# The first two gate/up steps of block 0, whole or in two token halves

## The chip, the cores and the metric

The kernel runs on one core of one Trainium2 chip. The metric is the device time of one execution in microseconds. A profile of one execution gives, for each engine, when every instruction began and how long it took; times inside it count from the start of its span. TensorE is called PE (its weight loads PEld), VectorE DVE, ScalarE ACT, GpSimd POOL, and the queue of SyncE that issues most transfers SP.

## The reference, cut to what matters

```python
xn = _layernorm(x)                                  # x: 2048 tokens x 512
B  = (_gelu(xn @ w_gate) * (xn @ w_up)) @ w_down    # w_gate, w_up: 512 x 1376
A  = 2 * Re(scan(Lam_bar, xn @ B_bar^T) @ Cmat^T) + xn * Dskip
return x + A + B
```

A state-space layer A (a complex linear recurrence over the 2048 tokens) and a gated feed-forward layer B read the same normalised input, and their sum is added to x.

## The kernel before

**Tiling.** The 2048 tokens are four blocks of 512, and a block is four token tiles of 128 (tile 0 to tile 3). `XNT[b]` holds the normalised block transposed, with the 512 features in four groups of 128 partitions. The 1376 columns of `w_gate` and `w_up` are steps of 128, numbered `ft` 0 to 10 (the last is 96 wide). A gate/up step (`GU`, line 844) is four matmuls of 128x512 for the gate and four for the up projection, one PSUM bank each; then ACT takes the gelu of the gate bank (line 859) and copies the up bank (863), and DVE multiplies the two (865).

**The start.** Block 0 does not wait for its own normalisation. `ks` and `GT_mm` (lines 702 and 713) run steps 0 to 6 of block 0 on centred but unscaled tokens, token tile by token tile: for tile `j` and column range `u` one bank takes gate and up side by side, and `GT_evac` scales both while it empties the bank, ACT with a gelu (line 722), then DVE with a product (725). A gelu writes one of three `GG` slots, which the product then frees. The last ten of these units are, in order, tile and range (3,0) in bank 6, (3,1) in 7, (0,2) in 0, (0,3) in 1, (1,2) in 2, (1,3) in 3, (2,2) in 4, (2,3) in 5, (3,2) in 0 and (3,3) in 7. Ranges 0 to 2 are 256 columns of gate and of up, range 3 is 128.

**Meanwhile** DVE normalises the four tiles of block 0 (line 635), and each is transposed into `XNT[0]` by a DMA of its own (`TR`, line 737), issued one behind the other on SP. Steps 7 to 10 of block 0, `GU(0, [7, 8, 9, 10])`, read `XNT[0]`: step 7 writes banks 2 and 3, step 8 banks 4 and 5, step 9 banks 6 and 7, and step 10 (line 818) banks 0 and 1. So a unit's bank must be emptied before the step that comes next in it.

**Other work at the start.** The layer's small parameters are loaded and transposed by a DMA (line 516). POOL raises e to one of them (558), DVE multiplies that by another (559, `th`), and from there DVE builds the phase tables (562 to 607). Block 1 is loaded, normalised and transposed (616 to 635, 737), `BU(0)` and `BU(1)` (line 750) multiply blocks 0 and 1 by the recurrence's input matrix; the first four units of `BU(1)` are already in two halves, tiles 0 and 1 first.

**What sets the order.** Each call adds an operation with an estimated duration to a list; what it must wait for follows from the buffers that it reads and writes. PE and SP keep the order of the calls. For DVE, ACT and POOL, a planner (`Sched.schedule`) chooses the order from the estimated durations, and it plans the whole kernel anew when one operation changes. Each engine then runs its list strictly as planned, with semaphore waits between engines. In a matmul's dependencies `XTr(b)` stands for the four tile transposes of a block:

```python
XTr = lambda b: XTk[b]
PE(f, d_pe([c1 - c0] * 4), wdeps(Wc, ft) + rd, [BANK[bank]], "GU%d" % b)
```

Of the kernel before, what the change touches and what calls it, by code (L numbers as in the profile page):

```python
# [348 lines left out]
NT, NB, KD, KP, KF = 16, 4, 4, 4, 11  # L349
# [6 lines left out]
def d_pe(n_list):  # L356
    return sum(n / 2.4 + 2.5 for n in n_list)
def d_dve_tt2x(n): return 100.0 + 0.52 * n
# [4 lines left out]
def d_act(n, ptr=0): return 190.0 + 0.833 * n + 90.0 * ptr  # L363
# [3 lines left out]
def build(nc, ins, out):  # L367
    with ExitStack() as es:
# [11 lines left out]
        WG = A.alloc("WG", [KD, F], BF16)  # L380
        WU = A.alloc("WU", [KD, F], BF16)
# [4 lines left out]
        WGc = [Buf("WGc%d" % i, "sbx", 10 * i, 10 * i + 1) for i in range(KD + 2)]  # L386
        WUc = [Buf("WUc%d" % i, "sbx", 100 + 10 * i, 101 + 10 * i) for i in range(KD + 2)]
# [30 lines left out]
        XTk = [[Buf("XT%d_%d" % (b, i), "xt", 4 * b + i, 4 * b + i + 1) for i in range(4)] for b in range(NB)]  # L418
        XT0 = XTk[0]
        XTr = lambda b: XTk[b]  # L420
# [128 lines left out]
        def next_bank():  # L549
            b_ = rstate["n"] % 8  # L550
            rstate["n"] += 1
            return b_
# [56 lines left out]
        def tables_act(after_gelu):  # L609
            t = ACT(lambda e: e.activation(SC16.ap, FRC.ap, ACTF.Sin, scale=SIN_SCALE), d_act(16) + 1300, [FRC], [SC16], "sin16", after=after_gelu)  # L610
            t = ACT(lambda e: e.activation(COST.ap, A1.ap, ACTF.Sin, bias=HPI.ap, scale=-SIN_SCALE), d_act(2048), [A1, HPI], [COST], "cost", after=[t])
            return ACT(lambda e: e.activation(SINT.ap, F1.ap, ACTF.Sin, scale=-SIN_SCALE), d_act(2048), [F1], [SINT], "sint", after=[t])  # L612
# [56 lines left out]
        def SKIP(b):  # L669
            for tt in range(4 * b, 4 * b + 4):  # L670
                xs = XN[tt % 8]
                V(lambda e, tt=tt, xs=xs: e.tensor_tensor(XD[tt].ap, xs.ap, DSKB.ap, ALU.mult),
                  d_dve_tt2x(512), [xs, DSKB], [XD[tt]], "skip")
# [156 lines left out]
            S.dma(lambda e: e.dma_start_transpose(HTt[k2][ft].ap.rearrange("p (j t) -> p j t", j=4), HR.ap),  # L830
                  1.2 * 128 * 1024, reads=HRp, writes=[HTt[k2][ft]], tag="tr_h%d" % b, issue=1200.0)

        def GU(b, fts=None):
            k2 = b % 2
            fts = list(range(KF) if fts is None else fts)
            banks = {}

            def mm(ft, W, Wc, bank, c0, c1, rd):
                m = FROWS[ft]

                def f(e):
                    ins_ = None
                    for dk in range(KD):
                        ins_ = e.matmul(PS[bank][0:m, c0:c1], W.ap[:, dk, 128 * ft:128 * ft + m], XNT[b].ap[:, dk, c0:c1],  # L844
                                        start=(dk == 0), stop=(dk == KD - 1))
                    return ins_
                PE(f, d_pe([c1 - c0] * 4), wdeps(Wc, ft) + rd, [BANK[bank]], "GU%d" % b)

            for ft in fts:
                m = FROWS[ft]  # L850
                if m < 128:
                    GU_rest(b)
                    continue
                banks[ft] = (next_bank(), next_bank())
                bg, bu = banks[ft]
                kk = (KF * b + ft) % 3
                for (W, Wc, bank) in zip((WG, WU), (WGc, WUc), banks[ft]):
                    mm(ft, W, Wc, bank, 0, 512, XTr(b))
                GATE["last_gelu"] = ACT(lambda e, bg=bg, kk=kk, m=m: e.activation(  # L859
                    GG[kk].ap[0:m, :], PS[bg][0:m, :], ACTF.Gelu_apprx_tanh),  # L860
                    d_act(512), [BANK[bg]], [GG[kk]], "gelu", after=GATE["before_gelu"])
                S.order_behind(GATE["last_gelu"], GATE.pop("evBu", None))
                ACT(lambda e, bu=bu, kk=kk, m=m: e.activation(UPB[kk].ap[0:m, :], PS[bu][0:m, :], ACTF.Copy),  # L863
                    d_act(512), [BANK[bu]], [UPB[kk]], "evU")
                V(lambda e, kk=kk, m=m, ft=ft, k2=k2: e.tensor_tensor(  # L865
                    HTt[k2][ft].ap[0:m, :], GG[kk].ap[0:m, :], UPB[kk].ap[0:m, :], ALU.mult),
                  d_dve_tt2x(512), [GG[kk], UPB[kk]], [HTt[k2][ft]], "hmul")
# [155 lines left out]
        LN(1, [0, 1]); LN(1, [2, 3])  # L1023
        TR(1)
        SKIP(0)
        GU(0, [7, 8, 9, 10])
        GATE["before_gelu"] = [tables_act([GATE["last_gelu"]])]
        SKIP(1)
        BU(0)
# [8 lines left out]
        late_loads()  # L1038
        scale_C()
        GU(1, [0, 1, 2, 10, 3, 4, 5, 6, 7, 8, 9])  # L1040
        BU(2)
        CHAIN(2)
        DN(0, True)
        LN_act(3); SKIP(3)
        GU(2, [0, 1, 2, 10, 3, 4, 5, 6, 7]); TR(3); GU(2, [8, 9])
        BU(3)
        CHAIN(3)
# [9 lines left out]
def bass_parallel_sum__ssm_conv_s5__geglu_ffn__prompt_kernel(  # L1057
    nc: bass.Bass,
    A_x: bass.AP,
    A_Lambda_re: bass.AP,  # L1060
    A_Lambda_im: bass.AP,
    A_B_re: bass.AP,
    A_B_im: bass.AP,
    A_C_re: bass.AP,
    A_C_im: bass.AP,
    A_log_dt: bass.AP,
    A_Dskip: bass.AP,
    B_x: bass.AP,
    B_w_gate: bass.AP,
    B_w_up: bass.AP,  # L1070
    B_w_down: bass.AP,
    out: bass.AP,
):
    ins = {
        "A_x": A_x, "A_Lambda_re": A_Lambda_re, "A_Lambda_im": A_Lambda_im,
        "A_B_re": A_B_re, "A_B_im": A_B_im, "A_C_re": A_C_re, "A_C_im": A_C_im,
        "A_log_dt": A_log_dt, "A_Dskip": A_Dskip,
        "B_w_gate": B_w_gate, "B_w_up": B_w_up, "B_w_down": B_w_down,
    }
    build(nc, ins, out)  # L1080
# [28 lines left out]
```

## Time and profile before

| What | Value |
|---|---|
| Median time of 3 runs | 177.01 us (176.86 to 177.09) |
| Span of the profiled execution | 176.4 us, 2522 instructions |
| Busy: DVE, ACT, POOL | 91%, 54%, 6% of the span |
| Granted TensorE clock | 1.00 |
| Matmuls of line 844 (gate/up steps) | 264, 58.1 us busy |
| Matmuls of line 713 (units of block 0) | 40, 7.1 us busy |
| DMA share in slices of 4.4 us, first nine | 5 9 9 8 9 9 9 4 9 tenths |

A busy PE in this profile is one that has matmuls in flight. The time of a 512-column matmul is given as 379 ns, though the next one begins 216 ns later: they overlap, and it is the distance between starts that counts.

### The profile page before, as it was taken

The numbers are of one execution on the slowest core, as the hardware profiler recorded it, in microseconds if no ns is written. First come the engines' busy times: TensorE is split into PE (matmuls) and PEld (weight loads), VectorE is DVE, ScalarE is ACT, GpSimd is POOL, SyncE is SP. The second block draws the span as 40 slices with busy tenths as digits, with TensorE's granted clock in tenths as the row PEclk, the third lists the DMA queues.
The fourth block names the chain that finished last, engine by engine and source line by source line (L and its number), as shares of the span: only waits on it lengthen the run. The fifth ranks groups of instructions, "written<-read, shape, count | busy, mean of one in ns | idle before, by whom it ended". The sixth has DMA issues, their size and how long they took to land.

```text
span 176.4 us, 2522 instructions
## 1 busy us (share of the span) xinstructions
PE 172.9 (98%) x889; PEld 84.8 (48%) x889; DVE 159.7 (91%) x279; ACT 96.0 (54%) x187; POOL 10.7 (6%) x24
## 2 busy tenths in 40 slices
PE   8999899999999999999999999999999999999995
PEld 2646364744644444444644444444464444444454
DVE  5987989997999989979899999989999899999941
ACT  5476577999766899292676693000667970000000
POOL 3212120202000000001200000000000000000000
DMA  5998999495998000001115000002001000000221
GB/s 176 256 334 139 248 202 157 94 162 104 193 288 226 4 0 2 0 30 59 33 32 103 16 0 0 4 0 86 33 0 30 4 0 0 0 0 0 91 93 61
DMA packets 32421, 14.37 MB, mean 81 GB/s; under 512 B 23736, under 2 KB 32408, under 8 KB 32408
## 3 DMA queue, kind: packets, MB, share of 16 engines
q1 hardware_dynamic: 32096, 13.94, 34.6%
q10 hardware_dynamic: 312, 0.27, 0.4%
q8 instruction: 7, 0.11, 0.3%
q14 instruction: 6, 0.05, 0.1%
HBM read 6.46 MB, written 2.10 MB: 49 GB/s over the span
## 4 chain that ended last, share of the span: by engine, by line
PE 95%; DMA 2%; DVE 1%; issue 0%
PE PS L885 37%; PE PS L844 32%; PE PS L750 16%; PE PS L702 3%; PE PS L818 3%; DMA arena<-arena 2%; PE PS L934 2%; PE PS L713 1%; DVE arena L725 1%; PE PS L685 1%; DVE arena L903 0%; PE PS L941 0%
## 5 line engine op out<-in xcount | busy, mean ns | idle before, releaser
L885 PE MATMUL PS<-arena 128*128 128x512 bf16 (+3 forms) x323 | 66.2, 366 | 0.0
L844 PE MATMUL PS<-arena 128*128 128x512 bf16 x264 | 58.1, 379 | 0.9 <-DMA arena<-arena 0.9
L885 PEld LDWEIGHTS PS<-arena 128*128 128x128 bf16 (+1 forms) x323 | 30.9, 98 | 35.2
L844 PEld LDWEIGHTS PS<-arena 128*128 128x128 bf16 x264 | 25.7, 98 | 31.4 <-issue 1.1
L788 DVE TENSOR_TENSOR_SCAN arena<-arena 128x512 bf16<-128x512 f32 x32 | 38.9, 1254 | 0.0
L859 ACT ACTIVATE arena<-PS 128x512 bf16<-128x512 f32 x33 | 19.8, 599 | 26.8 <-DVE arena L903 16.7
L750 PE MATMUL PS<-arena 128*128 128x512 bf16 (+1 forms) x144 | 28.2, 355 | 0.0
L863 ACT ACTIVATE arena<-PS 128x512 bf16<-128x512 f32 x33 | 19.8, 599 | 5.6 <-PE PS L844 5.6
L750 PEld LDWEIGHTS PS<-arena 128*128 128x128 bf16 x144 | 14.1, 98 | 13.3
L877 ACT ACTIVATE PS<-arena 128x512 f32<-128x512 bf16 (+2 forms) x17 | 9.6, 581 | 19.7 <-DVE arena L903 19.0
L759 ACT ACTIVATE arena<-PS 128x512 bf16<-128x512 f32 x32 | 17.5, 595 | 1.8 <-PE PS L750 1.8
L903 DVE TENSOR_TENSOR arena<-PS,arena 128x512 bf16<-128x512 f32 (+2 forms) x17 | 10.9, 653 | 6.4 <-PE PS L885 6.4
L865 DVE TENSOR_TENSOR arena<-arena 128x512 bf16<-128x512 bf16 x33 | 13.2, 417 | 2.7 <-ACT arena L863 2.5
L777 DVE TENSOR_TENSOR arena<-arena 128x4096 bf16<-128x4096 bf16 (+1 forms) x5 | 9.2, 1858 | 0.4 <-ACT arena L612 0.4
L800 DVE TENSOR_TENSOR arena<-arena 128x4096 bf16<-128x4096 bf16 x4 | 9.2, 2288 | 0.1
L775 DVE TENSOR_TENSOR arena<-arena 128x4096 bf16<-128x4096 bf16 (+1 forms) x5 | 9.2, 1857 | 0.0
L801 DVE TENSOR_TENSOR arena<-arena 128x4096 bf16<-128x4096 bf16 x4 | 9.1, 2284 | 0.0
L722 ACT ACTIVATE arena<-PS,arena 128x256 bf16<-128x256 f32 (+1 forms) x16 | 6.6, 449 | 4.1 <-PE PS L702 2.4
L616 DVE BATCH_NORM_STATS2 arena<-arena 128x6 f32<-128x512 bf16 x12 | 7.8, 680 | 0.2 <-DMA arena<-in_A_x_dram 0.2
L713 PE MATMUL PS<-arena 128*128 128x512 bf16 (+1 forms) x40 | 7.1, 336 | 0.0
L725 DVE SCALAR_TENSOR_TENSOR arena<-PS,arena 128x256 bf16<-128x256 f32 (+1 forms) x16 | 6.3, 444 | 0.5 <-PE PS L702 0.5
L702 PE MATMUL PS<-arena 128*128 128x512 bf16 (+1 forms) x30 | 6.3, 351 | 0.0
(95 smaller groups left out, 124.2 us busy)
## 6 DMA issues: line engine op xcount, KB each, us to landing
out_dram<-arena SPq DMA_DIRECT2D x15, 128.0 KB, 1.7
arena<-in_A_x_dram SPq DMA_DIRECT2D x3, 512.0 KB, 5.4
arena<-in_B_w_down_dram SPq DMA_DIRECT2D x1, 1280.0 KB, 7.1
arena<-in_B_w_gate_dram SPq DMA_DIRECT2D x4, 128.0 KB, 3.3
arena<-in_B_w_up_dram SPq DMA_DIRECT2D x4, 128.0 KB, 3.4
arena<-in_B_w_gate_dram SPq DMA_DIRECT2D x1, 480.0 KB, 6.7
arena<-in_B_w_up_dram SPq DMA_DIRECT2D x1, 480.0 KB, 7.5
arena<-arena SPq DMA_TRANSPOSE x25, 3.1
```

The costliest lines, as they stand in the source:

```text
L702: PE(lambda e: e.matmul(dst, XCd(j, k), WGU[:, ws[0]:ws[-1] + 1, k, f0:f1], start=first, stop=k == KD - 1, skip_group_check=True), d_pe([w ...
L750: ins_ = e.matmul(PS[bank][:, 128 * j0:128 * j1], BBT[c][dk].ap[:, 128 * s:128 * (s + 1)], XNT[b].ap[:, dk, 128 * j0:128 * j1], start=(dk ...
L759: GATE["evBu"] = ACT(lambda e, bank=bank, k3=k3, s=s, c=c: e.activation(SSc[k3][s][c].ap, PS[bank][:, :], ACTF.Copy), d_act(512), [BANK[ba ...
L775: V(lambda e, s0=s0, s1=s1: e.tensor_tensor(TA.ap[:, s0:s1], ssb.ap[:, s0:s1], cos4[:, s0:s1], ALU.mult), d_dve_tt2x(1024 * step), [ss, CO ...
L788: V(lambda e, g=g, rb=rb, init=init: e.tensor_tensor_scan(g.ap, rb, g.ap, init, ALU.mult, ALU.add), d_dve_scan(512), [g, PA[RRr]] + ([CARc ...
L844: ins_ = e.matmul(PS[bank][0:m, c0:c1], W.ap[:, dk, 128 * ft:128 * ft + m], XNT[b].ap[:, dk, c0:c1], start=(dk == 0), stop=(dk == KD - 1))
L859: GATE["last_gelu"] = ACT(lambda e, bg=bg, kk=kk, m=m: e.activation(GG[kk].ap[0:m, :], PS[bg][0:m, :], ACTF.Gelu_apprx_tanh), d_act(512), ...
L863: ACT(lambda e, bu=bu, kk=kk, m=m: e.activation(UPB[kk].ap[0:m, :], PS[bu][0:m, :], ACTF.Copy), d_act(512), [BANK[bu]], [UPB[kk]], "evU")
L865: V(lambda e, kk=kk, m=m, ft=ft, k2=k2: e.tensor_tensor(HTt[k2][ft].ap[0:m, :], GG[kk].ap[0:m, :], UPB[kk].ap[0:m, :], ALU.mult), d_dve_tt ...
L877: ACT(lambda e: e.activation(PS[bank][:, c0:c1], X[tt].ap[:, c0:c1], ACTF.Copy), d_act(c1 - c0), [X[tt]], [BANK[bank]], "seed")
L885: ins_ = e.matmul(PS[bank][:, c0:c1], l_[:, 128 * j:128 * (j + 1)], r_[:, c0:c1], start=False, stop=last and n == len(ops) - 1, skip_group ...
L903: V(lambda e: e.tensor_tensor(OUTB[ko].ap[:, c0:c1], PS[bank][:, c0:c1], XD[tt].ap[:, c0:c1], ALU.add), d_dve_1x(c1 - c0), [BANK[bank], XD ...
```

## The change

The first two gate/up steps of block 0, steps 7 and 8, are each cut into two halves by tokens. First the half of tiles 0 and 1 is computed for both steps (columns 0 to 255 of banks 2, 3, 4 and 5), then the half of tiles 2 and 3 (columns 256 to 511 of the same banks). Steps 9 and 10 and all other blocks stay whole. It is meant to let PE begin these steps once the transposes of tiles 0 and 1 are there, without waiting for that of tile 3.

```diff
-        def GU(b, fts=None):
+        def GU(b, fts=None, halved=()):
...
+            for h in range(2 if halved else 0):
+                for ft in halved:
+                    if h == 0:
+                        banks[ft] = (next_bank(), next_bank())
+                    for (W, Wc, bank) in zip((WG, WU), (WGc, WUc), banks[ft]):
+                        mm(ft, W, Wc, bank, 256 * h, 256 * h + 256, XTk[b][2 * h:2 * h + 2])
             for ft in fts:
...
-                banks[ft] = (next_bank(), next_bank())
+                kk = (KF * b + ft) % 3
+                if ft not in halved:
+                    banks[ft] = (next_bank(), next_bank())
+                    for (W, Wc, bank) in zip((WG, WU), (WGc, WUc), banks[ft]):
+                        mm(ft, W, Wc, bank, 0, 512, XTr(b))
                 bg, bu = banks[ft]
-                kk = (KF * b + ft) % 3
-                for (W, Wc, bank) in zip((WG, WU), (WGc, WUc), banks[ft]):
-                    mm(ft, W, Wc, bank, 0, 512, XTr(b))
...
-        GU(0, [7, 8, 9, 10])
+        GU(0, [7, 8, 9, 10], halved=(7, 8))
```

On PE the 16 matmuls of 128x512 of steps 7 and 8 become 32 of 128x256. Nothing else in the calls differs, but the planner orders DVE, ACT and POOL anew.

## The prediction

> **What bounds the kernel now.** I read the page's busy shares first, then PE's waits, then the chain that ended last, then the timeline around the one wait that this gives.
>
> ```profile
> PE 172.9 (98%) x889; PEld 84.8 (48%) x889; DVE 159.7 (91%) x279; ACT 96.0 (54%) x187; POOL 10.7 (6%) x24
> ```
>
> PE has matmuls in flight for 98% of the span, so only PE's idle time can be won. Its waits, longest first (total, times, longest):
>
> ```profile
> PE PS L844 <- DMA arena<-arena: 0.9, 1, 0.9
> PE PS L934 <- PEq L1094: 0.8, 1, 0.8
> ```
>
> The second is the program's start. The first is the only wait in the body, and the chain says which transfer ends it (start, duration):
>
> ```profile
> 14.34 4.24 DMA arena<-arena
> 18.58 0.14 issue
> 18.72 5.34 PE PS L844 x24
> 24.06 1.32 PE PS L818 x16
> 25.38 13.85 PE PS L750 x80
> ```
>
> From 18.72 to 174.6 us the chain is PE alone: what starts earlier at 18.72 ends earlier at the end, if no later wait opens. The timeline shows what runs before it:
>
> ```profile
> 10.42 5.19 SPq L737 DMA_TRANSPOSE arena<-arena  x4
> 10.77 7.09 PE L713 MATMUL PS<-arena 128*128 128x512 bf16 x40
> ...
> 12.66 2.31 DVE L725 SCALAR_TENSOR_TENSOR arena<-PS,arena 128x256 bf16<-128x256 f32 x6
> ...
> 15.03 1.02 POOL L558 TENSOR_TENSOR arena<-arena 128x4 bf16<-128x4 f32 x1 [5.42 <-DMA arena<-arena]
> ...
> 16.16 0.16 DVE L559 TENSOR_TENSOR arena<-arena 128x4 f32<-128x4 bf16 x1 [1.19 <-POOL arena L558]
> 16.26 0.74 DVE L725 SCALAR_TENSOR_TENSOR arena<-PS,arena 128x256 bf16<-128x256 f32 x2
> ...
> 18.72 5.34 PE L844 MATMUL PS<-arena 128*128 128x512 bf16 x24 [0.86 <-DMA arena<-arena]
> ```
>
> SP issues the four tile transposes 1.3 us apart from 10.42; by the view of line 737, cut to each, they land 4.7, 3.8, 3.1 and 4.2 us after their starts: 15.1, 15.5, 16.1 and 18.58. PE starts its last unit matmul at 17.59 and is free at 17.70. So tiles 0 and 1 have been there for 2.2 us when PE turns to step 7, and it stands until 18.72 for tile 3: 1.02 us between issue slots (0.86 in the waits, which count the drain). That is the most the change can bring. Note the second feature: DVE stands 1.19 us before line 559, whose input comes from POOL, which waited for the parameters' transpose (line 516; started 7.75, landed 7.1 later, 14.9).
>
> **What the skill says.** The Trainium skill, "TensorE: Matmul & The Clock Gate", section Back-to-back issue gap, gives 262 cycles for 256 columns and 518 for 512 as isolated gaps: two halves cost 6 cycles more than a whole. The trace agrees: line 713's starts are 0.108 us apart at 256 columns and 0.216 at 512, with a 98 ns weight load beside each. "Perfetto Trace Analysis", section Tensor Engine Instruction, calls ACT, DVE and GpSimd strict FIFOs. The trace agrees: the product for unit (1,2) started at 16.26 although its gelu had ended at 15.41; line 559 stood ahead of it. The same page, section DMA Instruction - HWDGE, says that a DMA's profiled time leaves out the data movement; here 1.27 us of issue against 4.24 to landing, so I use landings.
>
> **The change part by part.**
>
> *Removed:* the wait for tile 3 ahead of steps 7 and 8, 1.02 us. Tiles 2 and 3 are now needed 1.7 us later (four half groups of 4 x 0.108), at 19.4 or after, when they have landed.
>
> *Added on PE:* 16 more matmuls and weight loads; from 0.108 against 0.216 the columns cost the same, so nothing.
>
> *Added as a wait, by the shorter steps:* banks 4 and 5 (units (2,2) and (2,3)) are needed after two half groups, 0.86 us, not after two whole ones. Before, the product for (2,2) ended at 18.00 and bank 4 was wanted at 20.45: no issue as DVE was ordered then.
>
> *Moved, and this decides:* the planner orders DVE and ACT anew. In the built program ACT first empties the tile 3 transposes (line 690) and then starts the gelus. PE issues those transposes until 9.69; with 0.27 us from PE to ACT, as from line 702 to the first gelu, line 690 starts at 9.96, and the first gelu at 10.44 (0.48 behind, as before) instead of 9.73. Its product starts at 11.03 instead of 10.32. Then come six more products (0.39 to 0.40 each), one normalisation (0.32) and one reciprocal (0.12), so the 7th product ends at 14.3, where the 8th had ended before. And line 559 now stands behind the 7th, where it stood behind the 10th. It still cannot start before 16.16 (landing 14.90 + 0.13 + POOL 1.02 + 0.11). So units (3,0), (0,2) and (0,3), done by 14.96 before, wait for it:
>
> | DVE after line 559 | starts | ends | why |
> |---|---|---|---|
> | (0,2) | 16.26 | 16.74 | 0.10 behind line 559, as before |
> | (3,0) | 16.66 | 17.13 | 0.40 a product |
> | (1,2) | 17.05 | 17.53 | the same |
> | (0,3) | 17.69 | 18.03 | its gelu needs the GG slot of (3,0): 17.13 + 0.08 + 0.37 + 0.11 |
> | line 562, (1,3) | 17.95 | 18.37 | 0.08, then 0.34 |
> | line 603 | 18.29 | | 0.26 behind |
> | (2,2) | 18.69 | 19.17 | its gelu needs the slot of (0,3): 18.03 + 0.08 + 0.47 + 0.11 |
>
> PE queues behind these. Unit (3,2) reuses bank 0, which (0,2) frees at 16.74; with 0.06 from DVE to PE (as at 3.69 to 3.75, line 962 to 685) it starts at 16.80, not 16.40: 0.40 lost, with all of PE behind it. It and (3,3) take 1.30, two half groups 0.86: PE reaches bank 4 at 18.96 and finds it free at 19.23: 0.27 more. Bank 5 follows in time, 0.40 later on DVE against 0.43 on PE. Six half groups (0.432 each) end at 21.82. Before, four whole groups from 18.72 ended at 22.18.
>
> Sum: -1.02 + 0.40 + 0.27 = -0.35 us by the parts, 22.18 - 21.82 = 0.36 by the ends: 177.01 - 0.36 = 176.65.
>
> *Further moves.* In block 1 the normalisation of tile 7 is now behind four table products (line 605, 0.66 each): 29.1 instead of 25.6. Its transpose is issued at about 29.6 and with the 3.05 it took before (27.51 to 30.56) lands at 32.6. `BU(1)` wants tiles 6 and 7 at 33.84 - 0.36 = 33.5: hidden by 0.7 to 0.9, where it was 3.3. The transfers behind it on SP come some 2.6 us later; PE needs none of them before 57 us, hidden behind line 844 of block 1. POOL's start order changes within 2.3 us, ahead of the first input's landing at 2.94: no cost.
>
> **The rivals.**
> - *The full gain, 176.0.* The banks are free in time and PE runs through: 17.70 + 8 x 0.432 = 21.16, 1.02 less. For it: only 0.5 us of earlier parameters suffice for most of it. Against it: the landing at 14.90 stands in a full DMA row (8 to 9 tenths).
> - *A new wait of equal size, 177.1.* PE's time now hangs on the parameters' landing plus a fixed chain, before on tile 3's landing; in the trace these lie 3.68 us apart. If parameters land 0.5 later, each of the table's rows moves with them: 0.36 - 0.5, slightly slower or the same. For it: nothing in DVE's list lies between to absorb it. Against it: SP and its transfers are unchanged up to there.
> - *Slower, 177.6.* The transpose of tile 7 takes 4.7 us, as tile 0's did: 29.6 + 4.7 + 0.14 = 34.4 against 33.5, 0.95 lost. For it: the margin shrinks from 3.3. Against it: the DMA row is down to 4 tenths from 30.9 on, and 3.05 was measured there.
>
> **How the numbers follow.** Chances: forecast 0.50, full gain 0.19, equal wait 0.18, slower 0.13. The threshold of 0.2% is 0.35 us, on which the forecast sits; I give 0.36 of its 0.50 to faster and 0.14 to the same, leaning to faster because the two added waits are priced with every latency at its full measured size. The equal wait gives 0.14 to the same and 0.04 to slower. Faster 0.55, same 0.28, slower 0.17. The range goes from the full gain to just past the equal wait, 176.0 to 177.3, leaving out most of the slow case.
>
> **What would show it.** In the changed profile: PE waits on DVE line 725 at about 16.8 (line 713, 0.3 to 0.4) and about 19.2 (line 844, 0.2 to 0.3), and no wait on a DMA; line 559 at 16.1 to 16.2 with the idle before it near 1.9; the first gate/up matmul near 18.1; line 818 near 23.5 instead of 23.9. It is wrong if PE's first wait is gone with nothing in its place, if line 558 starts away from 15.0, or if line 750 waits near 33.5.

## The result and the profile after

The changed kernel took 177.71 us (median of 6 runs, 177.65 to 178.20) where the kernel before took 176.90 us (6 runs, 176.58 to 177.09): a ratio of 1.0052, 95% interval 1.0037 to 1.0066. It is slower by some 0.8 us. Timed again beside the experiments it gave 1.0032 (1.0012 to 1.0052).

The page's busy shares hardly move:

```profile
PE 172.1 (97%) x890; PEld 86.2 (49%) x905; DVE 158.6 (90%) x279; ACT 95.1 (54%) x187; POOL 9.9 (6%) x24
```

PE's waits do. The wait of line 844 for a transfer is gone, and line 713, which had none, waits for DVE (total, times, longest):

```profile
PE PS L713 <- DVE arena L725: 0.9, 1, 0.9
PE PS L941 <- PEq L1101: 0.8, 1, 0.8
```

The chain that ended last, cut to the start of the kernel, says where that wait comes from (start, duration; `...` marks lines left out). On PE, where matmuls overlap, a piece of the chain begins when the last matmul of the piece before has ended, up to 0.16 us after its own first matmul has started. The text uses the starts, from the timeline.

```profile
7.67 7.79 DMA arena<-arena
15.46 0.02 issue
15.48 0.02 POOLq L342
15.50 0.10 issue
15.60 1.03 POOL arena L558
...
16.72 0.06 DVE arena L559
16.78 0.04 issue
16.82 0.49 DVE arena L725
17.32 0.14 issue
17.45 1.46 PE PS L713 x8
18.92 0.87 PE PS L844 x8
19.79 0.05 issue
19.84 2.78 PE PS L844 x24
```

Read from the top: the parameters' transpose (line 516, from 7.67) lands at 15.46, POOL's line 558 follows, then DVE's line 559, then the product for unit (0,2) (line 725, 16.82 to 17.32), and only then PE may write bank 0 again, for unit (3,2). In the kernel before, the chain ran through the transpose of tile 3, and line 559 was nowhere on it. PE had been ready since 16.36, so it lost 1.09 us between issue slots (0.94 in the waits view, which counts the drain). The second wait is at 19.84: bank 4, held by unit (2,2), whose product ends at 19.69. The matmul before it started at 19.52, 0.32 us earlier instead of 0.11, so another 0.2 us is lost; most of it hides in the chain behind the end of that matmul.

The timeline of DVE shows the long stand ahead of line 559 and what queues behind it (start, duration, in brackets the idle time before and what ended it):

```profile
12.26 1.65 DVE L725 SCALAR_TENSOR_TENSOR arena<-PS,arena 128x256 bf16<-128x256 f32 x4
16.72 0.16 DVE L559 TENSOR_TENSOR arena<-arena 128x4 f32<-128x4 bf16 x1 [2.81 <-POOL arena L558]
16.82 1.72 DVE L725 SCALAR_TENSOR_TENSOR arena<-PS,arena 128x256 bf16<-128x256 f32 x4
```

DVE does nothing for 2.81 us, and the four products behind line 559 are the ones that empty banks 0, 6, 2 and 1. That is the mechanism that the prediction described, with a larger wait than it priced.

What comes later in the kernel adds little: in all twelve profiles of this study, of every kernel, the time of the execution less the start of its first matmul of line 818 is 153.8 to 154.0 us. So what separates the kernels is nearly all settled ahead of line 818, which starts at 24.18 here and at 23.89 in the profile before.

What the result asks is why the sum came out on the other side: what had been gained at tile 3, and whether the new place of line 559 is the whole of the loss.

### The profile page after: what moved, and what is told of

The parts are those of the page before. It is cut to its first block, busy times and chain, and to the rows that moved or that the text cites. A ratio compares the mean times of both kernels' runs of the same rounds, so it can differ in the third digit from the quotient of the medians.

```text
span 176.9 us, 2532 instructions
## 1 busy us (share of the span) xinstructions
PE 172.1 (97%) x890; PEld 86.2 (49%) x905; DVE 158.6 (90%) x279; ACT 95.1 (54%) x187; POOL 9.9 (6%) x24
## 4 chain that ended last, share of the span: by engine, by line
PE 88%; DMA 4%; SPq 4%; issue 1%; POOL 1%; DVE 0%; DVEq 0%; POOLq 0%
PE PS L892 37%; PE PS L844 32%; PE PS L750 16%; DMA arena<-arena 4%; PE PS L818 3%; SPq L489 2%; SPq L494 1%; PE PS L713 1%; POOL arena L558 1%; SPq L498 0%; DVE arena L725 0%; DVE arena L910 0%; DVE arena L559 0%; SPq L342 0%; DVEq L342 0%
## 5 line engine op out<-in xcount | busy, mean ns | idle before, releaser
L844 PE MATMUL PS<-arena 128*128 128x512 bf16 (+1 forms) x274 | 57.8, 367 | 0.4
L844 PEld LDWEIGHTS PS<-arena 128*128 128x128 bf16 x280 | 27.3, 98 | 29.0 <-ACT arena L722 0.3
L750 PE MATMUL PS<-arena 128*128 128x512 bf16 (+1 forms) x141 | 27.8, 355 | 0.2
L750 PEld LDWEIGHTS PS<-arena 128*128 128x128 bf16 x144 | 14.1, 98 | 13.3
L713 PE MATMUL PS<-arena 128*128 128x512 bf16 (+1 forms) x40 | 7.4, 336 | 1.0 <-DVE arena L725 0.9
L702 PE MATMUL PS<-arena 128*128 128x512 bf16 (+1 forms) x30 | 6.0, 337 | 0.1
```

The costliest lines, as they stand in the source:

```text
L750: ins_ = e.matmul(PS[bank][:, 128 * j0:128 * j1], BBT[c][dk].ap[:, 128 * s:128 * (s + 1)], XNT[b].ap[:, dk, 128 * j0:128 * j1], start=(dk ...
```

## The experiments

**Theories.** P (plan): the planner's new place for line 559, ahead of products that free banks and behind a transfer that lands late, makes the loss. L (landings): the wait for tile 3 in the first profile was not usual, so the change had little to win. Rivals: H, the halves themselves cost; D and R, other parts of the new order on DVE and ACT cost.

**The kernel before, profiled again.** No edit.

> The kernel before, unchanged, profiled once more. Theory P (plan): the changed kernel is slower because the planner put line 559 ahead of three products that empty banks, and line 559 waits for the parameters' transpose. Theory L (landings): on top of that, the wait for tile 3 that the first profile showed (0.86 us) is larger than in the usual execution, since landings move from one execution to the next. Time within 0.2% of before under every theory. Under L the tile 3 transpose lands clearly before 18.58 us and PE waits less than 0.5 us for it; under P alone the wait is near 0.9 us again.

It measured 0.9998 (0.9986 to 1.0011) against itself. The chain of this execution, in the same stretch as before:

```profile
10.89 6.93 PE PS L713 x40
17.82 0.05 issue
17.87 5.13 PE PS L844 x23
```

PE goes from line 713 into line 844 without a wait; the waits view has no line for a transfer any more. (One matmul record is missing here, x23 of 24, so PE began at 17.66.) Tile 3's transpose was issued at 14.36, at the same time as in the first profile, and landed 2.5 us later, at 16.86 instead of 18.58. This execution took 176.63 us; the first profiled one took 177.68. This is as L expected: the wait that the change removes is absent here.

A third profile, of a single execution, asks how usual that is:

> The kernel before, profiled a third time, to see how usual the wait for tile 3 is. L: tile 3 lands near 16.9 us and PE does not wait for it, as in the second profile; else it lands past 18 us again with a wait of 0.5 us or more.

Tile 3 landed at 16.82, PE did not wait, and the execution took 176.77 us. In the eleven profiles of this study other than the first, of all kernels, tile 3 landed between 16.43 and 17.04; 18.58 stands alone. What the wait is worth over many executions, the next experiment says.

**The halves with the old order.** The diff of the change, plus (the lists of `PLAN` are left out; they give the old place of each instruction):

```diff
         S.schedule()
+        PLAN = {...}                         # DVE, ACT and POOL: the order of the kernel before
+        for e_, at in PLAN.items():
+            made = [op for op in S.ops if op.eng == e_]
+            S.order[e_] = [made[k] for k in at]
```

> The two steps in halves, but DVE, ACT and POOL run their lists in the order of the kernel before. P: PE does not wait before the gate/up halves nor in line 713, so the kernel is faster than before by what tile 3 costs there: 0.9 us (0.5%) if the first profile is typical, 0.0 to 0.5 us under L. Theory H (the halves themselves cost, by 16 more matmuls and weight loads or by banks 4 and 5 being wanted sooner): as slow as the changed kernel, +0.3 to +0.7%.

1.0005 (0.9987 to 1.0022), and no wait at lines 713 or 844 in its chain:

```profile
11.66 6.93 PE PS L713 x40
18.58 3.49 PE PS L844 x32
```

H is out, and so is a gain above 0.13%. From the first gate/up matmul to the first of line 818 it is 5.22 us here and 5.17 in the first profile of the whole steps: the halves cost 0.05 us. Since this kernel wants tile 3 only 1.7 us later, the two together, 0.23 and 0.05 us, also bound what the wait for tile 3 is usually worth: some 0.3 us.

**Whole steps with the new order.** The kernel before with the same lines, and the changed kernel's order in `PLAN`.

> Whole steps as before, but DVE, ACT and POOL run in the order that the planner made for the changed kernel. P: slower than before by 0.2 to 0.9 us (0.1 to 0.5%), with PE waiting in line 713 for line 725 near 17 us; some 0.2 us faster than the changed kernel, because bank 4 is not wanted early. H: within 0.2% of before.

1.0032 (1.0015 to 1.0048), without a single half step in it. Its waits:

```profile
PE PS L934 <- PEq L1102: 0.8, 1, 0.8
PE PS L713 <- DVE arena L725: 0.5, 1, 0.5
PE PS L702 <- DMA arena<-in_B_w_up_dram: 0.4, 1, 0.4
```

The second is the changed kernel's wait. The third is a wait for weights near 5.4 us; it stands in four of the twelve profiles, the third one of the kernel before among them, with 0.2 to 0.6 us. The order alone makes most of the loss.

**One instruction moved back.** The changed kernel, with line 559 four products later on DVE, behind that of unit (0,3):

```diff
         S.schedule()
+        row = S.order["vector"]
+        th = [op for op in row if op.tag == "th"][0]      # line 559
+        row.remove(th)
+        done = [n for n, op in enumerate(row) if op.writes and op.writes[0].name == "H0_0_3"]
+        row.insert(done[0] + 1, th)
```

> The changed kernel with one instruction moved on DVE: line 559 stands behind the product for unit (0,3) instead of ahead of the one for (0,2). P: PE's wait in line 713 is gone, 1.0 us or more faster than the changed kernel, so 0.0 to 0.5% faster than before. Theory D (the loss comes from the rest of the new order, such as the transpose of tile 7 being issued 3 us later): as slow as the changed kernel, 0.3 to 0.7% slower than before.

0.9994 (0.9973 to 1.0015). Its chain:

```profile
11.27 6.93 PE PS L713 x40
18.20 3.49 PE PS L844 x32
21.70 0.05 issue
21.75 1.67 PE PS L844 x7
```

All 40 matmuls of line 713 and all 32 half ones of line 844 run without a gap, the wait at bank 4 included. Everything else of the new order is still in it, so D is out as the source of the 0.3 to 0.7% that it expected; a cost within the interval's 0.15% would not show.

**The same instruction moved up in the kernel before.** As above, with unit (3,0) for (0,3), in whole steps and the old order: line 559 now stands ahead of the products of (3,1), (0,2) and (0,3). Run twice.

> The kernel before with whole steps and its own order, but with line 559 moved up on DVE by three products, to stand behind the product of unit (3,0) and ahead of those of (3,1), (0,2) and (0,3). P: this place alone makes the loss: line 559 starts near 16.2, the product of (0,2) ends near 17.2, bank 0 comes free 0.75 us after PE wants it, and the time rises by 0.5 to 0.8 us (0.3 to 0.45%). Theory R (the rest of the new order, such as line 690 going ahead of the first gelu, is needed for the loss): less than 0.2% from before.

> The kernel with line 559 moved up by three products, timed once more because its first interval (0.9996 to 1.0033) left no change possible. P: 0.2 to 0.45% slower than before, less where PE comes late to line 713, since PE then wants bank 0 later; R: less than 0.2%.

The first gave 1.0015 (0.9996 to 1.0033), which by itself decides nothing; the second 1.0031 (1.0017 to 1.0046). The medians are 177.54 and 177.57 us, and that of the 26 executions together is 177.55, against 177.03 for the 63 fast ones of the kernel before beside them. In both profiles line 559 starts at 16.25, the product of (0,2) at 16.76, and PE waits for it in line 713:

```profile
PE PS L713 <- DVE arena L725: 0.4, 1, 0.4
PE PS L713 <- DVE arena L725: 0.6, 1, 0.6
```

So the one place is enough for the wait, with line 690 and the gelus where they were. R said that it would not be; the times alone do not shut R out, since it allowed up to 0.2%, but the two traces do. It cost a little less than the 0.75 us expected, because PE came to line 713 at 11.23 and 11.03 here, 0.3 to 0.5 us later than in the first profile, and wanted bank 0 later.

**A larger dose.** The same with six products behind line 559.

> The kernel before with line 559 moved up on DVE by six products instead of three: behind the normalisation of tile 3 and ahead of the product of unit (2,0), which frees bank 4. P: the loss grows with the number of products that stand behind line 559: it starts near 16.2 us, bank 4 comes free near 16.9, 1.4 to 1.8 us after PE wants it, and bank 0 another 0.3 us late, so the time rises by 1.5 to 2.1 us (0.85 to 1.2%). Theory R (the place of line 559 is a side issue): within 0.3% of before.

1.0105 (1.0085 to 1.0124), inside what was expected. Its waits and the head of its chain:

```profile
PE PS L713 <- DVE arena L725: 1.1, 1, 1.1
```

```profile
14.72 1.03 POOL arena L558
...
15.84 0.06 DVE arena L559
15.90 0.04 issue
15.95 0.49 DVE arena L725
16.44 0.14 issue
16.57 1.46 PE PS L713 x8
18.04 0.10 issue
18.14 1.46 PE PS L713 x8
19.60 0.05 issue
19.65 5.13 PE PS L844 x23
```

Here it is unit (2,2), bank 4, that starts late, at 16.57, and the cost has risen from 0.3% with three products moved behind line 559 to 1.05% with six. It is not the count alone: the three more include the product that empties bank 4, which PE wants at 15.29, 1.3 us before it would want bank 0.

**Take the wait away instead.** The changed kernel in its own order, but the parameters' transpose goes out two loads earlier (its order on DVE, ACT and POOL is held by `PLAN` lines as above):

```diff
         load_par()
-        load_W()
         tr_par()
+        load_W()
```

> The changed kernel with its own order on DVE, ACT and POOL, but on SP the parameters' transpose (line 516) is issued ahead of the last two weight loads (line 494) instead of behind them. P: the parameters land 1.5 us or more earlier, line 559 waits less or not at all where the planner put it, PE's wait in line 713 is gone, and the time is within 0.2% of before. If the place of line 559 costs whenever its input comes: as slow as the changed kernel, +0.4 to +0.6%. A third way, in which P is not tested: the two weight loads land after 18 us and PE waits for them in line 844.

0.9999 (0.9979 to 1.0019). The timeline has POOL and DVE at:

```profile
11.76 1.02 POOL L558 TENSOR_TENSOR arena<-arena 128x4 bf16<-128x4 f32 x1 [1.40 <-DMA arena<-arena]
14.43 0.16 DVE L559 TENSOR_TENSOR arena<-arena 128x4 f32<-128x4 bf16 x1
```

The parameters land at 11.62, no line of the waits view names line 713 or 844, and line 559 runs at 14.43 with no idle time before it, in the very place where it cost 2.81 us of DVE. The weights landed at 14.78, still in time. The place costs only because of the landing that it waits for.

**The changed kernel again.**

> The changed kernel again, timed and profiled beside the others. P: 0.4 to 0.6% slower than before, with PE waiting 0.4 us or more in line 713 for line 725 and again 0.1 to 0.3 us at bank 4; the second wait is what it has over the whole steps in the same order, so 0.1 to 0.2% slower than that kernel's 1.0032.

1.0032 (1.0012 to 1.0052), less than the 0.4 to 0.6% expected. In this profile the wait at bank 0 is nearly gone (0.07 us), also against what was expected: the parameters landed at 14.94 and PE came to line 713 at 11.23 instead of 10.50, so it wanted bank 0 only at 16.85. The wait at bank 4 is 0.2 us again. The loss at bank 0 therefore moves between executions, from under 0.1 to 1.1 us, and where it is small, PE has already been late.

PE comes to line 713 anywhere from 10.50 to 11.49 us. Much of that is PE's pace ahead of it. Here are matmuls of line 702 in the first profile of the changed kernel, then the same in this one (the last line of each begins the 512-column matmuls):

```profile
4.48 0.38 PE L702 MATMUL PS<-arena 128*128 128x256 bf16 x2
5.29 1.05 PE L702 MATMUL PS<-arena 128*128 128x256 bf16 x8
6.39 1.03 PE L702 MATMUL PS<-arena 128*128 128x512 bf16 x4
```

```profile
4.50 0.58 PE L702 MATMUL PS<-arena 128*128 128x256 bf16 x2
5.79 1.27 PE L702 MATMUL PS<-arena 128*128 128x256 bf16 x8
7.12 0.38 PE L702 MATMUL PS<-arena 128*128 128x512 bf16 x1
```

Two matmuls of 128x256 begin 108 to 120 ns apart in the first from 4.48 us on; here they begin up to 214 ns apart, and 109 only after 6.3 us. That is 0.71 of the 0.73 us between the two arrivals. In other profiles the wait for weights near 5.4 us comes on top or takes its place. An early PE meets bank 0 still full, a late one does not. The late arrival by itself does not separate the kernels: with line 559 moved back and with the parameters first, PE came to line 713 at 11.11 and 11.10, and their times are those of before.

An estimate for the usual execution follows. Whole steps without a wait take 12.11 us from the first matmul of line 713 to that of line 818 (second and third profile of the kernel before), and 153.8 us follow, so the median of 177.05 us (54 executions of the kernel before) means an arrival near 11.1, if PE waits for nothing. In the changed kernel, with this profile's landing of the parameters, that leaves some 0.2 us at bank 0, to which 0.2 at bank 4 and 0.05 for the halves come: near the 0.5 us between the medians here (177.58 and 177.07).

The second wait was expected to put this kernel 0.1 to 0.2% above the whole steps in the new order; both ratios are 1.0032. So the share of the second wait in the loss is shown by the traces alone (0.2 us in both profiles of the changed kernel, none in the whole steps), not by the times.

## Why the prediction was wrong

**The step that failed is the first term of the sum, -1.02 us for the wait at tile 3.** The trace showed it, and it was read rightly, but it belonged to that one execution. Tile 3 landed at 18.58 there and at 16.86 and 16.82 in the next two, where PE was ready at 17.66 and 17.79. The usual worth of the term is near nothing: the halves in the old order bound it at some 0.3 us. With it the full-gain rival had no ground either. A sign was at hand and not used: the profiled execution took 177.68 us where the timed runs had a median of 177.01. The surplus of 0.67 us does not name its cause, but it said that this execution was not the usual one; the two later profiled executions, without the wait, took 176.63 and 176.77.

**Without that term the working gives 0.40 + 0.27 = 0.67 us slower**, beside 0.81 measured (177.71 - 176.90) and 0.3 to 0.5% in the two ratios. That it comes so near is partly luck, since the 0.40 was found anywhere from 0.07 to 1.09. The other steps, one by one:

- *Line 559 behind the 7th product, and bank 0 waiting for it:* right, and shown by moving line 559 in both directions. Priced at 0.40, it was 1.09 in the profile after: the parameters landed at 15.46 instead of 14.90, which put line 559 0.56 later (16.72 against 16.16), DVE to PE took 0.14 and not 0.06, and PE wanted the bank 0.04 earlier. PE would have wanted it 0.27 earlier, having come to line 713 at 10.50 and not 10.77, but unit (0,2) began 0.24 late at 12.46, just after a weight load had landed at 12.37. The other profile of the same kernel had 0.07: the prediction had no term for when PE comes to line 713.
- *Bank 4:* priced at 0.27, found at 0.2 in both.
- *The halves at no cost:* right to 0.05 us.
- *Tile 7 of block 1:* right. Its transpose was issued at 30.2 and landed at 32.8, and line 750 waits nowhere. The rival that ended slower, at 177.6, named this transfer; it had the sign and nearly the measured 177.71 by luck, without the cause.
- *The equal-wait rival:* it had the right chain, time hanging on the parameters' landing, and in the profile after they did land 0.56 later, but it weighed that against a gain of 1.02 that was not there.

The range failed because all of its cases took the tile 3 wait as given.

## What to carry to other kernels

Before a wait of under 1% is priced from one profile, compare that execution's time with the timed runs, or take a second profile; a wait that hangs on one transfer's landing may be that execution's alone. When a planner reorders in-order engines, look first for the instruction with the latest input, at what stands behind it, and at when the next engine wants the buffers that this work frees: that, and not the edit itself, set the cost here. Such an instruction is cheap to fix at either end, by moving it behind the work that frees buffers or by issuing its transfer earlier; here each brought the time back to that of before (0.9994 and 0.9999).

## What the hardware showed unexpectedly

The same 128x512 transpose, issued at 14.34 and 14.36 us in two executions of one program, landed 4.24 and 2.50 us later; what delayed the first one stays open. The issue of the parameters' transpose (line 516) took between 1.81 and 2.85 us on SP in the changed kernel's and the moved-back kernel's profiles, and 1.17 us when it went out ahead of the last two weight loads.

PE reached its full pace at different times in executions of one program: by 4.48 us in the first profile of the changed kernel, at some 6.3 in the second. What sets the moment was not tried.
